# Clustered attention and a gated layer: fp16 hi/lo halves for the cluster logits of pairs 1 to 3, with a new order of pieces

## The chip, the cores and the metric

The kernel runs on one core of a Trainium2 chip. The metric is the device time of one execution in microseconds (us); lower is better. A core has five engines that run side by side and wait for one another through semaphores: TensorE (PE, matmuls into PSUM), VectorE (DVE), ScalarE (ACT), GpSimd (POOL) and SyncE (SP, which here only issues DMAs). Each engine takes its own instructions strictly in the order in which the program issued them.

## The reference

Four batches of eight heads, 768 positions, head dimension 64. Each query and each key is assigned to the nearest of 16 centroids of its head, by the largest cosine; a query sees only the keys of its own cluster. The result, with the heads side by side, is the input of a gated layer.

```python
q_assign = np.argmax(np.einsum('bhsd,hcd->bhsc', q_n, c_n), axis=-1)
k_assign = np.argmax(np.einsum('bhsd,hcd->bhsc', k_n, c_n), axis=-1)
mask = q_assign[:, :, :, None] == k_assign[:, :, None, :]
scores = np.where(mask, scale * np.matmul(q, k.transpose(0, 1, 3, 2)), -1e9)
attn = softmax(scores)                  # rows
x = (attn @ v).transpose(0, 2, 1, 3).reshape(3072, 512)
out = (1 / (1 + np.exp(-(x @ w_gate))) * (x @ w_val)) @ w_out     # 512 -> 1536 -> 512
```

q, k, v and the weights come as fp32. An argmax depends only on the direction of a query, so q and k need not be divided by their norms; but it needs more than fp16's precision where two centroids are close.

## The kernel before, in words

**Heads, pairs and steps.** Heads are worked in pairs (b, p), p from 0 to 3. The attention is a sequence of 384 steps, 96 for each batch. In a step, `do_scores` multiplies one block of 128 keys with 384 queries (`sc`, one PSUM bank of the four of `ring`), and ACT takes the exp of it (`es`, L554). Some steps later, `do_av` multiplies `es` with the values (`av`, L567; `ahead` is 4 in the first batch). At a head's end DVE and POOL divide by the row sums (`normalise`), and the result goes to `xT`, turned by PE or by a DMA.

**The mask is in the matmul.** The tile `T` of a head has 80 rows: 64 of q and k, turned so that the head dimension lies on the partitions, and 16 rows of one-hot cluster numbers. On the key side such a row is 1 in the key's cluster, on the query side it is a large negative number in every cluster but the query's own. So a score of unequal clusters comes out very negative, and exp makes it 0.

**Two ways to the cluster numbers.** The first batch has no time for the slow way, and turns q and k on PE in fp32 (`head`): `f_turn` (`t`, L691, three turns of 128x128 for each head and side, two positions of 64 numbers in each), `f_copy` (`e`, to the fp32 tile `T32`), `f_logits` (`g`, L720, fp32 matmuls with the block-diagonal centroids `cbd`), and `f_half` (`h`, L683, two fp16 casts of 64 partitions from `T32` into `T`). Then `PT`/`PA`/`PB` (L732, L738) find the maximum and mark it, `TT` turns the one-hot rows on PE (L402), and `d` places them in `T` (L749, L751). Batches 1 to 3 (`pair_prep`) split each number into two fp16 halves, hi (L852, a cast) and lo (L858, the number less hi), side by side in a tile `hl`; a DMA transposes `hl` into `T`, so that hi and lo lie under each other, and the logits are fp16 matmuls with the centroids' own hi and lo (`cm`, L352), of which a copy and an addition make the sum (L358, L381).

**Order.** The order of issue is written out by hand in the table `A`. Each piece of work has a name and a place in steps (negative: ahead of the first step; in `pair_prep`, counted from the pair's own first step). `item` puts a piece at the later of its own place and those of the pieces that it builds on; `run_bg(n)` issues the pieces of step n after its scores. A name with an E at the end gives the engine: D is DVE, P is POOL, A is ACT. `dum` are matmuls of zeros that keep PE running at the start, `dn` how many. `w` and `wo` are the weights' loads, which POOL issues; q, k, v are loaded through SP's queue, into four buffers each.

**PSUM.** `prep_bank` takes one of two banks (`op`) for turns, one-hots and value sums as long as the gated layer hasn't begun (before step 96); `bank` takes one of `ring`, which scores and logits share.

**The gated layer.** `ffn_push` queues the layer's matmuls for half a batch (`g` L420, `v` L435, `o` L452), and `ffn_run` spreads them between the steps. The first half of the first batch is due at step 80; what is left runs after the last step.

Of the kernel before, what the change touches and what calls it, by code (L numbers as in the profile page):

```python
# [9 lines left out]
HP = mybir.dt.float16  # L10
# [6 lines left out]
def kernel(  # L17
# [35 lines left out]
    hlp = pool("hl", 4)  # L53
# [21 lines left out]
    def prep_bank(n=512, dt=FP, name="bank"):  # L75
# [9 lines left out]
        "1.0.h00": -54.3, "1.0.l00": -66.6, "1.0.h01": -55.4, "1.0.l01": -60.7, "1.0.tn0": -55.3,  # L85
        "1.0.lg0": -29.3, "1.0.pk00": -62.4, "1.0.pk01": -48.1, "1.0.pk02": -43.9,
        "1.0.pk03": -35.1, "1.0.h10": -50.9, "1.0.l10": -66.6, "1.0.h11": -48.2,
        "1.0.l11": -58.4, "1.0.tn1": -49.0, "1.0.lg1": -25.5, "1.0.pk10": -30.8,
        "1.0.pk11": -58.2, "1.0.pk12": -61.1, "1.0.pk13": -50.3, "1.0.otpe": 0, "1.0.ot": -9.4,
        "1.0.oc": -39.2, "1.0.hop0": -60.3, "1.0.hop1": 1.4, "1.0.vc": -32.4, "1.0.vsm": -19.0,  # L90
        "1.0.vsa": -36.7, "1.0.vsb": -16.9, "1.0.vsr": 1.5, "1.1.ldk": -64.3, "1.1.ldq": -71.6,
        "1.1.ldv": -31.0, "1.1.h00": -40.3, "1.1.l00": -35.9, "1.1.h01": -37.2, "1.1.l01": -84.0,
        "1.1.tn0": -27.6, "1.1.lg0": -20.3, "1.1.pk00": -20.2, "1.1.pk01": -39.9,
        "1.1.pk02": -19.8, "1.1.pk03": -20.7, "1.1.h10": -39.0, "1.1.l10": -31.1,
        "1.1.h11": -36.5, "1.1.l11": -46.2, "1.1.tn1": -22.7, "1.1.lg1": -16.3,
        "1.1.pk10": -14.1, "1.1.pk11": -25.3, "1.1.pk12": -39.8, "1.1.pk13": -46.7,
        "1.1.otpe": 0, "1.1.ot": -12.4, "1.1.oc": -7.2, "1.1.hop0": -34.8, "1.1.hop1": -13.6,
        "1.1.vc": -45.9, "1.1.vsm": -33.5, "1.1.vsa": -26.6, "1.1.vsb": -2.7, "1.1.vsr": 11.6,
        "1.2.ldk": -56.8, "1.2.ldq": -74.0, "1.2.ldv": -49.0, "1.2.h00": -67.9, "1.2.l00": -56.0,
        "1.2.h01": -61.1, "1.2.l01": -48.3, "1.2.tn0": -37.8, "1.2.lg0": -19.8,  # L100
        "1.2.pk00": -29.9, "1.2.pk01": -16.6, "1.2.pk02": -33.0, "1.2.pk03": -19.0,
        "1.2.h10": -37.0, "1.2.l10": -32.1, "1.2.h11": -60.1, "1.2.l11": -34.3, "1.2.tn1": -29.9,
        "1.2.lg1": -15.8, "1.2.pk10": -17.4, "1.2.pk11": -30.5, "1.2.pk12": -15.7,
        "1.2.pk13": -25.1, "1.2.otpe": 0, "1.2.ot": -28.0, "1.2.hop0": -24.1, "1.2.hop1": -29.9,
        "1.2.vc": -46.6, "1.2.vsm": -26.4, "1.2.vsa": -1.2, "1.2.vsb": -19.0, "1.2.vsr": 8.1,
        "1.3.ldk": -73.1, "1.3.ldq": -70.8, "1.3.ldv": -86.1, "1.3.h00": -71.8, "1.3.l00": -72.4,
        "1.3.h01": -61.5, "1.3.l01": -51.2, "1.3.tn0": -49.1, "1.3.lg0": -35.6,
        "1.3.pk00": -36.6, "1.3.pk01": -59.5, "1.3.pk02": -51.9, "1.3.pk03": -30.3,
        "1.3.h10": -53.4, "1.3.l10": -40.6, "1.3.h11": -55.4, "1.3.l11": -55.9, "1.3.tn1": -75.1,
        "1.3.lg1": -20.4, "1.3.pk10": -25.4, "1.3.pk11": -37.4, "1.3.pk12": -18.3,  # L110
        "1.3.pk13": -18.4, "1.3.otpe": 0, "1.3.ot": -11.6, "1.3.hop0": -13.3, "1.3.hop1": -20.5,
        "1.3.vc": -26.2, "1.3.vsm": -11.5, "1.3.vsa": -26.9, "1.3.vsb": -28.2, "1.3.vsr": 4.0,
        "lag0": 8, "lag1": 14, "x0": 56.6, "1.0.h00E": 'P', "1.0.l00E": 'P', "1.0.h01E": 'D',
        "1.0.l01E": 'P', "1.0.h10E": 'P', "1.0.l10E": 'P', "x1": 55.5, "1.0.h11E": 'D',
        "1.0.l11E": 'P', "1.0.mkE": 'P', "x2": 49.1, "1.1.h00E": 'D', "1.1.l00E": 'D',
        "1.1.h01E": 'P', "1.1.l01E": 'P', "1.1.h10E": 'D', "1.1.l10E": 'D', "x_last": 4,
        "1.1.h11E": 'D', "1.1.l11E": 'D', "reserve": 5000, "1.2.h00E": 'P', "1.2.l00E": 'P',
        "1.2.h01E": 'D', "1.2.l01E": 'D', "1.2.h10E": 'D', "1.2.l10E": 'D', "1.1.mkE": 'P',
        "1.2.h11E": 'P', "1.2.l11E": 'D', "1.3.h00E": 'D', "1.3.l00E": 'P', "1.3.h01E": 'P',
        "1.3.l01E": 'D', "1.2.mkE": 'D', "1.3.h10E": 'P', "1.3.l10E": 'D', "1.3.h11E": 'P',  # L120
        "1.3.l11E": 'P', "1.3.mkE": 'P', "cena": -39.3, "cenb": -42.1, "cenc": -30.2,
        "exp": -27.1, "cend": -28.2, "cene": -7.9, "t00": -34.1, "e00": -44.7, "g00": -28.2,
        "h000": -31.3, "h001": -35.4, "t01": -35.1, "e01": -70.3, "g01": -32.3, "h010": -35.2,
        "h011": -15.9, "pt0": -45.6, "pm00": -25.6, "pm01": -34.0, "tt0": -50.1, "pl00": -20.6,
        "pl010": -33.9, "pl011": -28.3, "t10": -29.6, "e10": -11.5, "g10": -29.0, "h100": -10.0,
        "h101": -4.9, "t11": -23.3, "e11": -3.4, "g11": 2.2, "h110": -11.6, "h111": -38.5,
        "pt1": -40.4, "pm10": 7.4, "pm11": -27.2, "tt1": -26.2, "pl10": -10.6, "pl110": -15.2,
        "pl111": -1.5, "vc0": -30.8, "vs0": 12.8, "t20": 10.4, "e20": -22.8, "g20": 14.4,
        "t21": 9.0, "e21": -29.3, "g21": 11.6, "h220": -12.6, "h221": -1.8, "t30": -2.0,
        "e30": -25.3, "g30": 9.3, "t31": 5.6, "e31": -7.3, "g31": 14.5, "h320": -18.3,  # L130
        "h321": -7.6, "PT1": -3.3, "PA1": 2.9, "PB1": 2.6, "TT1": 19.1, "direct1": 2,
        "d100": -14.6, "d101": 3.1, "d110": -13.8, "d111": -48.3, "vc1": 11.3, "vs1": 17.1,
        "t40": 21.3, "e40": 4.0, "g40": 30.2, "t41": 27.5, "e41": 15.1, "g41": 36.0,
        "h420": 14.0, "h421": 36.5, "t50": 30.5, "e50": 36.7, "g50": 44.2, "t51": 30.1,
        "e51": 33.5, "g51": 21.7, "h520": 27.4, "h521": 36.8, "PT2": 46.5, "PA2": 13.2,
        "PB2": 10.0, "TT2": 39.9, "direct2": 2, "d200": -45.4, "d201": -10.1, "d210": -50.1,
        "d211": -5.0, "vc2": 32.1, "vs2": 51.1, "t60": 42.5, "e60": 37.6, "g60": 47.5,
        "t61": 44.8, "e61": 31.4, "g61": 48.3, "h620": 57.1, "h621": 41.7, "t70": 43.0,
        "e70": 31.0, "g70": 49.0, "t71": 39.8, "e71": 26.7, "g71": 52.4, "h720": 41.6,
        "h721": 33.2, "PT3": 38.3, "PA3": 37.5, "PB3": 56.2, "TT3": 35.7, "direct3": 2,  # L140
        "d300": -29.5, "d301": -8.8, "d310": -20.2, "d311": 22.7, "vc3": 51.8, "vs3": 65.5,
        "e00E": 'D', "e01E": 'A', "h000E": 'A', "h001E": 'P', "h010E": 'D', "h011E": 'D',
        "pl00E": 'D', "pl010E": 'P', "pl011E": 'P', "vc0E": 'A', "e10E": 'A', "e11E": 'A',
        "h100E": 'D', "h101E": 'D', "h110E": 'P', "h111E": 'A', "pl10E": 'D', "pl110E": 'D',
        "pl111E": 'P', "cut": 2, "e20E": 'A', "e21E": 'D', "e30E": 'A', "e31E": 'D', "vc1E": 'P',
        "h220E": 'P', "h221E": 'P', "h320E": 'P', "h321E": 'P', "e40E": 'D', "e41E": 'A',
        "e50E": 'D', "e51E": 'D', "vc2E": 'P', "h420E": 'P', "h421E": 'P', "h520E": 'D',
        "h521E": 'D', "e60E": 'A', "e61E": 'A', "e70E": 'D', "e71E": 'D', "vc3E": 'P',
        "h620E": 'P', "h621E": 'P', "h720E": 'A', "h721E": 'P', "xm2E": 'D', "xm3E": 'A',
# [8 lines left out]
        "dum0": -40, "dum1": -30.5, "dum2": -27.9, "dum3": -33.5, "dum4": -31.5, "dum5": -33,  # L158
        "dum6": -27.6, "dum7": -30.9, "dum8": -23.6, "dum9": -20, "dum10": 6.2, "dum11": -0.9,
        "dum12": 0.1, "dn0": 12, "dn1": 0, "dn2": 2, "dn3": 1, "dn4": 0, "dn5": 3, "dn6": 4,  # L160
        "dn7": 3, "dn8": 3, "dn9": 3, "dn10": 1, "dn11": 0, "dn12": 0,
# [228 lines left out]
    def new_oh():  # L390
        oh_n[0] += 1
        return ohs[oh_n[0] % 3]
# [140 lines left out]
    def rows(s):  # L533

        b, p, e = s["b"], s["p"], s["e"]
        if b:
            return {(b, p, f"hop{e}")}
        h = 2 * p + e
        if p == 0:
            i = s["c0"] // 3  # L540
            return {f"h{h}{x}{y}" for x in range(2) for y in range(2)} | {
                f"pl{e}0", f"pl{e}10", f"pl{e}1{i}"}
        d = {f"d{p}{e}{x}" for x in range(2)} if e < A.get(f"direct{p}", 2) else {f"hop{p}{e}"}
        return d | {f"h{h}20", f"h{h}21"}
# [191 lines left out]
    def f_mark(h, nh, s, oh):  # L736
# [3 lines left out]
            bcast(mx[:, :, 6 * s : 6 * s + 6], NCL), ALU.is_lt if s else ALU.is_equal,  # L740
        )

    def place(t, ps, slot, c0, n, key, eng):
        src = ps[32 * slot : 32 * slot + 16, 0 : n * 128].rearrange("p (c t) -> p c t", t=128)
        dst = t[64:80, c0 : c0 + n, :]
        if eng is ACT:
# [250 lines left out]
```

## Time and profile before

| | us |
|---|---|
| median of 5 runs | 340.16 (339.14 to 342.49) |
| the profiled execution | 339.52 |
| its span, first to last instruction | 337.5 |
| first exp / first matmul of the gated layer | 13.44 / 53.89 |
| last step's exps / end of the layer | about 280 / 334 |

Busy time of the engines by stretch, in us:

| stretch | PE | DVE | ACT | POOL |
|---|---|---|---|---|
| 0 to 10 | 7.2 | 4.7 | 5.5 | 3.8 |
| 10 to 50 | 38.2 | 28.7 | 32.3 | 23.6 |
| 50 to 110 | 57.4 | 38.5 | 48.6 | 22.3 |

Lines of the profile name the engine, the line of the kernel, the operation and the tiles. A time in a fence is the start in the span or a length, both in us, and the text ahead of each says which; in groups of instructions the mean is in ns. A bracket at the end, or the last column of a group, tells how long the engine stood idle before the instruction and which other instruction ended that. The granted TensorE clock is 1.00 in every stretch.

### The profile page before, as it was taken

The page shows a single profiled execution, that of the slowest core. Times are in us where ns is not written, and L with a number is a line of the kernel's source. Part 1 is how long each engine was busy: PE and PEld are TensorE (multiplying, and loading weights), DVE is VectorE, ACT ScalarE, POOL GpSimd, SP SyncE. Part 2 cuts the span into 40 slices and gives each one's busy share as a digit, 9 for nine tenths or more (in the row PEclk, how much of TensorE's full clock was granted, in tenths as well). Part 3 has the DMA queues.
Part 4 walks back from the last instruction along what each step waited for, and adds up shares of the span by engine and source line. Part 5 has one row for each costly group of instructions (what it writes and reads, how often), then busy time and mean ns, then how long its engine had stood idle before and what let it go on. Part 6 is the DMA issues. An engine that isn't in the chain of part 4 may idle for free.

```text
span 337.5 us, 8262 instructions
## 1 busy us (share of the span) xinstructions
PE 324.1 (96%) x3135; PEld 208.3 (62%) x3135; DVE 173.4 (51%) x428; ACT 231.6 (69%) x537; POOL 110.4 (33%) x196
## 2 busy tenths in 40 slices
PE   7899999979999998999999999999999999999995
PEld 6688866656656665566665666566655665654552
DVE  4657788666754755465454746465442433403230
ACT  4779799868878886678776877778776873322330
POOL 4365834344043554334444243444120110000000
PEclk9999999999999999999999999999999999999999
DMA  7999997985969594869395837433331200002102
GB/s 256 304 259 249 205 156 198 247 138 112 228 84 235 122 213 105 231 180 142 84 251 130 227 78 198 113 72 81 81 84 40 60 14 14 0 31 81 77 0 93
DMA packets 80854, 46.17 MB, mean 137 GB/s; under 512 B 61104, under 2 KB 77744, under 8 KB 80816
## 3 DMA queue, kind: packets, MB, share of 16 engines
q1 hardware_dynamic: 76816, 40.55, 51.1%
q0 software_dynamic: 3712, 4.72, 7.9%
q8 instruction: 24, 0.39, 0.5%
q10 hardware_dynamic: 288, 0.39, 0.3%
q14 instruction: 14, 0.11, 0.1%
HBM read 28.34 MB, written 6.29 MB: 103 GB/s over the span
## 4 chain that ended last, share of the span: by engine, by line
PE 88%; DMA 5%; ACT 2%; DVE 2%; issue 1%; SPq 0%; POOL 0%; ACTq 0%
PE g L420 18%; PE v L435 18%; PE o L452 18%; PE sc L549 17%; PE av L567 9%; PE lg L720 3%; DMA T<-hl 3%; PE lg L352 2%; DMA vraw<-in_v_dram 2%; DMA T<-ohT 1%; PE t_ps L691 1%; ACT es L554 1%; PE oh_ps L402 0%; ACT L783 0%; DVE oh L738 0%
## 5 line engine op out<-in xcount | busy, mean ns | idle before, releaser
L554 ACT ACTIVATE es<-sc 128x384 f16<-128x384 f32 x384 | 171.5, 499 | 41.5 <-PE sc L549 27.9
L549 PE MATMUL sc<-T 80*128 80x384 f16 x384 | 115.4, 327 | 3.1 <-DMA T<-ohT 1.3
L567 PEld LDWEIGHTS <-es 128*128 128x128 f16 x1152 | 81.6, 98 | 45.1 <-issue 1.5
L440 DVE SCALAR_TENSOR_TENSOR hT<-th,v 128x384 f16<-128x384 f32 x96 | 52.9, 552 | 93.5 <-PE av L567 49.9
L567 PE MATMUL av<-va,es 128*128 128x65 f16 x1152 | 97.4, 193 | 0.6 <-ACT es L554 0.5
L420 PE MATMUL g<-xT,wg 128*128 128x384 f16 x384 | 78.1, 325 | 0.1
L435 PE MATMUL v<-xT,wv 128*128 128x384 f16 x384 | 78.1, 325 | 0.0
L452 PE MATMUL o<-wo,hT 128*128 128x512 f16 x288 | 71.1, 378 | 0.7 <-ACT ob L461 0.7
L426 ACT ACTIVATE th<-g 128x384 f32<-128x384 f32 x96 | 47.3, 492 | 34.0 <-PE g L420 16.7
L327 POOL TENSOR_TENSOR xp<-t,rec 128x384 f16<-128x384 f32 (+1 forms) x38 | 26.7, 703 | 109.1 <-DVE rec L326 99.1
L420 PEld LDWEIGHTS <-wg 128*128 128x128 f16 x384 | 37.2, 97 | 21.5 <-issue 0.4
L435 PEld LDWEIGHTS <-wv 128*128 128x128 f16 x384 | 37.3, 97 | 21.2 <-issue 0.7
L452 PEld LDWEIGHTS <-hT 128*128 128x128 f16 x288 | 28.0, 97 | 26.3 <-issue 1.0
L549 PEld LDWEIGHTS <-T 80*128 80x128 f16 x384 | 37.7, 98 | 2.9 <-DMA T<-ohT 1.1
L325 DVE TENSOR_TENSOR t<-av,sv 128x390 f32<-128x390 f32 (+1 forms) x42 | 19.4, 463 | 13.4 <-PE av L567 13.4
L878 POOL TENSOR_SCALAR oh<-oh 128x96 f16<-128x96 f16 x22 | 9.9, 452 | 32.2 <-DVE oh L370 26.5
L284 DVE TENSOR_REDUCE vs<-vraw 128x64 f16<-128x384 f32 x24 | 19.5, 814 | 0.0
L858 POOL TENSOR_TENSOR hl<-qraw,hl 128x384 f16<-128x384 f32 x20 | 18.3, 913 | 2.1 <-DVE hl L852 0.6
L461 ACT ACTIVATE ob<-o 128x512 f32<-128x512 f32 x16 | 9.6, 597 | 13.6 <-PE o L452 13.5
L381 DVE TENSOR_TENSOR lgs<-lg,lglo 128x192 f32<-128x192 f32 x24 | 8.5, 355 | 15.4 <-ACT lglo L358 15.1
L858 POOL TENSOR_TENSOR hl<-kraw,hl 128x384 f16<-128x384 f32 x12 | 11.0, 913 | 8.6 <-DVE hl L852 7.8
L720 PE MATMUL lg<-cbd,T 128*128 128x32 f32 x96 | 12.8, 273 | 0.7 <-DVE cbd L263 0.5
(81 smaller groups left out, 219.5 us busy)
## 6 DMA issues: line engine op xcount, KB each, us to landing
vraw<-in_v_dram SPq DMA_DIRECT2D x16, 384.0 KB, 4.9
out_dram<-ob SPq DMA_DIRECT2D x24, 256.0 KB, 2.3
kraw<-in_k_dram SPq DMA_DIRECT2D x15, 384.0 KB, 4.4
qraw<-in_q_dram SPq DMA_DIRECT2D x15, 384.0 KB, 6.1
wg<-in_moe_w_gate_dram POOLq DMA_DIRECT2D x2, 768.0 KB, 14.9
wv<-in_moe_w_val_dram POOLq DMA_DIRECT2D x2, 768.0 KB, 20.2
wo<-in_moe_w_out_dram POOLq DMA_DIRECT2D x4, 384.0 KB, 18.9
T<-ohT SPq DMA_DIRECT2D x48, 24.0 KB, 1.9
```

The lines of the kernel that those rows point to most:

```text
L284: DVE.tensor_reduce(s[:, e, 0:64], RAW["v", b, p][:, e].rearrange("p c d -> p d c"), AX.X, ALU.add)
L327: eng.tensor_tensor(x, t[..., 0:64], bcast(r, 64), ALU.mult)
L420: PE.matmul(out=g[:, 0:n], lhsT=wg[fc // WQ][:, dc, fc % WQ, :], rhs=xT[:, dc, t0 : t0 + n], start=(dc == 0), stop=(dc == NDC - 1),)
L426: ACT.activation(th[:, 0:n], g[:, 0:n], AF.Tanh, scale=0.5)
L435: PE.matmul(out=w[:, 0:n], lhsT=wv[fc // WQ][:, dc, fc % WQ, :], rhs=xT[:, dc, t0 : t0 + n], start=(dc == 0), stop=(dc == NDC - 1),)
L440: DVE.scalar_tensor_tensor(hT[:, fc, 0:n], st[0][:, 0:n], 1.0, w[:, 0:n], ALU.add, ALU.mult)
L452: PE.matmul(out=o, lhsT=hT[:, fc, bass.ts(t, 128)], rhs=wo[fc // 3][:, fc % 3, :], start=(fc == 0), stop=(fc == NFC - 1),)
L549: PE.matmul(out=sc.rearrange("p (c t) -> p c t", t=128), lhsT=s["k"], rhs=s["q"], start=True, stop=True,)
L554: ACT.activation(es, sc, AF.Exp, scale=SCALE)
L567: PE.matmul(out=av[:, s["c0"] - base + i, :], lhsT=s["es"][:, bass.ts(i, 128)], rhs=VA[b, p][:, e, s["j"], :], start=(first and i == 0), s ...
L720: PE.matmul(out=st0[lgk(h)][:, o : o + 2 * NCL], lhsT=t32(h, s)[:, c, :], rhs=cbd[:, h], start=True, stop=True,)
L858: eng.tensor_tensor(hl[:, :, 64:128], RAW["kq"[side], b, p][:, e], hl[:, :, 0:64], ALU.subtract)
```

## The change

Pairs 1 to 3 of the first batch get a third way (`style1` to `style3`, all 1), in place of `head`: hi and lo as in the later batches, but turned by PE in fp16, six turns for each head and side, one copy out of PSUM straight into `T`, and logits with the centroids' hi and lo summed in PSUM, two matmuls of 16 columns for each 128 positions. `T32` and the halves `h` are not needed for these pairs. Pair 0 keeps its fp32 way.

```diff
-    hlp = pool("hl", 4)
+    hlp = pool("hl", 5)
...
+    def hi(h, c0, c1, eng):
+        if ("hl", h) not in st0:
+            st0["hl", h] = hlp.tile([128, 12, 128], HP, tag="hl", name="hl")
+        r = RAW["kq"[c0 // 6], 0, h // 2][:, h % 2, c0 % 6 : c0 % 6 + c1 - c0]
+        (ACT.copy if eng is ACT else eng.tensor_copy)(st0["hl", h][:, c0:c1, 0:64], r)
+
+    def lo(h, c0, c1, eng):
+        hl = st0["hl", h][:, c0:c1]
+        r = RAW["kq"[c0 // 6], 0, h // 2][:, h % 2, c0 % 6 : c0 % 6 + c1 - c0]
+        eng.tensor_tensor(hl[:, :, 64:128], r, hl[:, :, 0:64], ALU.subtract)
+
+    def turn_a(name, h, c0, n, bk):
+        if (0, h) not in T:
+            T[0, h] = tp.tile([128, 12, 128], HP, tag="T", name="T")
+        ps = st0[name] = bk(NCH * 128, HP, name="t_ps")
+        for i in range(n):
+            PE.transpose(ps[:, bass.ts(i, 128)], st0["hl", h][:, c0 + i, :], identh)
+
+    def turn_b(name, h, c0, n, eng):
+        (ACT.copy if eng is ACT else DVE.tensor_copy)(
+            T[0, h][:, c0 : c0 + n, :].rearrange("p c t -> p (c t)"),
+            st0[name][:, 0 : n * 128],
+        )
+
+    def a_logits(p, s, e):
+        if ("lgA", p) not in st0:
+            st0["lgA", p] = bank(512, name="lg4")
...
+        for c in range(6):
+            for i in range(2):
+                PE.matmul(
+                    out=lg[:, bass.ts(12 * s + 6 * e + c, NCL)], lhsT=t[:, 6 * s + c, :],
+                    rhs=cm[:, h, i, :], start=(n == c == i == 0), stop=(i == 1),
+                    skip_group_check=True,
+                )
...
+    def a_pick(p, s):
+        lg = st0["lgA", p][:, 0:384].rearrange("p (c n) -> p c n", n=NCL)
+        if s == 0:
+            st0["oh", p] = new_oh()
+            st0["mxA", p] = top(lg)
+        mark(lg, st0["mxA", p],
+             [(12 * s, 12 * s + 12, 2, s == 0, oh_view(st0["oh", p], s, 2, 2, 6))])
```

The pieces are named with pair, side and head: `H` hi, `L` lo, `T` turn, `E` copy, `G` logits, so `H100` is hi of pair 1, side k, head 0. Their places and engines in the table are new, and nearly all other places and many engines change with them; of those, the ones that the prediction speaks of:

```diff
-        "e00E": 'D', "e01E": 'A', "h000E": 'A', "h001E": 'P', "h010E": 'D', "h011E": 'D',
-        "h100E": 'D', "h101E": 'D', "h110E": 'P', "h111E": 'A', "pl10E": 'D', "pl110E": 'D',
+        "e00E": 'A', "e01E": 'D', "h000E": 'P', "h001E": 'P', "h010E": 'P', "h011E": 'A',
+        "h100E": 'A', "h101E": 'D', "h110E": 'A', "h111E": 'D', "pl10E": 'P', "pl110E": 'A',
...
-        "vc1E": 'P', "vc2E": 'P', "vc3E": 'P', "xm3E": 'A',
+        "vc1E": 'A', "vc2E": 'A', "vc3E": 'P', "xm3E": 'P',
...
-        "dn0": 12, "dn5": 3, "dn6": 4, "dn7": 3, "dn8": 3, "dn9": 3, "dn10": 1,
+        "dn0": 11, "dn5": 1, "dn6": 1, "dn7": 1, "dn8": 2, "dn9": 2, "dn10": 0,
...
+        "H100": -19, "L100": -16.0, "H101": -6.1, "L101": -8.6, "H110": -13.1, "L110": -17.5,
+        "H111": -7.1, "L111": -18.5, "T100": 6.5, "E100": 5, "G100": 8.5, "T101": 8.5,
+        "E101": 9.1, "G101": 10, "T110": 8.5, "E110": 10, "G110": 11, "T111": 9.5, "E111": 11, "G111": 13,
...
+        "H100E": 'A', "H101E": 'P', "L100E": 'P', "L101E": 'P', "H110E": 'D', "H111E": 'D',
+        "L110E": 'P', "L111E": 'P', "E100E": 'A', "E101E": 'D', "E110E": 'D', "E111E": 'D',
+        "H200E": 'D', "H201E": 'A', "L200E": 'P', "L201E": 'D', "H210E": 'A', "H211E": 'D',
+        "L210E": 'P', "L211E": 'P', "E200E": 'D', "E201E": 'D', "E210E": 'A', "E211E": 'D',
+        "H300E": 'P', "H301E": 'P', "L300E": 'P', "L301E": 'P', "H310E": 'A', "H311E": 'D',
+        "L310E": 'P', "L311E": 'P', "E300E": 'A', "E301E": 'D', "E310E": 'D', "E311E": 'D',
```

Pair (1,0), the first of the next batch, has its hi pieces h00 and h10 and its lo piece l10 moved from POOL to DVE and its h01 from DVE to POOL; pairs (1,1) to (1,3) have nine pieces moved from DVE to POOL and one the other way.

## The prediction

> **What bounds the kernel now.** I read the busy shares first. TensorE is busy 96% of a 337.5 us span, so the first question is what it is busy with where the change is made. The projections begin at 53.89 us (first `g` matmul, step 80 of the attention), so I took busy times from the first exp (13.44) to there: span, then PE, PEld, DVE, ACT, POOL, the clock, the DMA share and GB/s.
>
> ```profile
> PE 324.1 (96%) x3135; PEld 208.3 (62%) x3135; DVE 173.4 (51%) x428; ACT 231.6 (69%) x537; POOL 110.4 (33%) x196
> 13.44:53.70 40.26, 38.36 (x496) 31.45 (x495) 29.25 (x71) 34.65 (x87) 24.06 (x38) 1.00 1.16 222
> ```
>
> Two engines are nearly full there: PE 38.36 and ACT 34.65 of 40.26 us. The chain that ended last gives prices on PE's path (start, length, what), free of the overlap of pipelined matmuls, and PE's timeline gives the fp16 logits that batch 1 already uses:
>
> ```profile
> 18.31 0.36 PE t_ps L691 x3
> 18.93 0.67 PE lg L720 x6
> 23.70 0.34 PE oh_ps L402 x6
> ...
> 48.34 0.45 PE L352 MATMUL lg<-cm,T 128*128 128x32 f16 x12
> 48.64 0.32 PE L549 MATMUL sc<-T 80*128 80x384 f16 x1
> ```
>
> Three fp32 turns take 0.36 us (0.12 each), six records of fp32 logits 0.67 (0.112 each), six fp16 turns 0.34 (0.057 each), and twelve fp16 logits hold the next score up from 48.34 to 48.64 (0.025 each). Then ACT alone, by groups in the same stretch and in its timeline:
>
> ```profile
> L554 ACT ACTIVATE es<-sc 128x384 f16<-128x384 f32 x79 | 33.3, 527 | 5.5 <-PE sc L549 5.1 <-PE av L567 0.2
> 22.26 5.25 ACT L554 ACTIVATE es<-sc 128x384 f16<-128x384 f32 x13 [0.98 <-PE sc L549]
> ```
>
> Thirteen exps back to back take 5.25 us, 0.404 each, though one alone lasts 0.499: an ACT instruction in a stream costs some 0.095 less than its duration. Eighty exps need 32.3 us of 40.26 whatever PE does. ACT idles 5.6 us, 5.1 of them waiting for scores: that is what a faster PE can give back.
>
> Last the two ends of this stretch: PE's wait for the first one-hot turn, and the longest transfer of the chain after step 80.
>
> ```profile
> 9.98 0.50 PE L772 MATMUL oh_ps<-identh,oh 128*64 128x128 f16 x6 [0.79 <-ACT T L683]
> 72.45 0.47 PE L352 MATMUL lg<-cm,T 128*128 128x32 f16 x12 [1.34 <-DMA T<-hl]
> ...
> 63.77 8.64 DMA T<-hl
> ```
>
> **The change part by part.**
>
> *TensorE.* Removed for three pairs: 36 fp32 turns at 0.12 = 4.3 us and 72 records of fp32 logits at 0.112 = 8.1, together 12.4. Added: 72 fp16 turns at 0.057 = 4.1 and 144 fp16 logits at 0.025 = 3.6 (16 columns where the row has 32; I take no discount), together 7.7. PE's path loses 4.6 us before step 80. Eleven warm-up matmuls also go; all but one stand before the first score, where the chain holds three of them (0.43 us).
>
> Here the Trainium skill speaks against the change. "TensorE: Matmul & The Clock Gate", Part 4 (PE-mode transpose), says that a 128x128 turn takes about 275 ns in a kernel, and that turns don't count as work for the clock. By that rule 72 turns cost 19.8 us in place of 4.1: PE would lose nothing and gain 11 us, near 351 us for the kernel. The row says 0.34 us for six of them in a stream with scores on both sides, at a granted clock of 1.00 in every stretch; each record does last 220 ns, but they overlap. I take the row.
>
> *The engines that feed it.* Nearest rows: hi on POOL 0.53, on DVE 0.39 to 0.56, on ACT 0.51 (its 64x384 cast); lo on POOL 0.913, on DVE 0.56; a 768-wide fp16 copy out of PSUM on DVE 0.551 (the 16x768 one-hot copy), on ACT 0.834 (its 128x768 cast). With the engines of the new table:
> - before: ACT 5 copies + 1 half = 3.3 us; DVE 7 copies + 2 halves = 5.8; POOL 9 halves = 7.6
> - after: ACT 4 hi + 3 copies = 4.5; DVE 5 hi + 1 lo + 9 copies = 7.9; POOL 3 hi + 11 lo = 11.6
>
> The values of pairs 1 and 2 move from POOL to ACT, 2 x 0.834. DVE also takes over two casts and a lo of pair (1,0) and gives one cast away, about +0.9. So DVE goes from 29.3 to about 32.3 us of the stretch, POOL from 24.1 to about 25. I cost both at nothing: they stay below PE and ACT. Without that cover, if one in-order queue made a turn late, the price would be its own added 3 us on DVE, or 4 on POOL.
>
> A second rule bears here. "SBUF — State Buffer" (Who interferes with whom) has a DVE cast in a two-port mode and a GpSimd instruction exclude each other for a whole instruction. The trace agrees: the DVE cast at 34.10 lasts 0.83 us beside POOL's 0.83 us product from 33.89, where a cast of kraw mostly lasts 0.35. By the rule, five hi on DVE could each last 0.83: 2 us more, 34.5 of some 39. Still cover, so both sums are the same.
>
> *ACT, the step that decides.* In the stretch it now has, beside the exps: copies E100, E210, E300 and casts vc1, vc2 (5 x 0.834), hi H201, H210, H310 (3 x 0.51), the one-hot part pl110 (taken as 0.48) and two lglo copies as before (0.65 together): 6.8 us less 11 x 0.095 = 5.8. With 32.3 for the exps it is 38.1, against 34.65 now. PE's need on the chain's prices is 37.0 now (80 steps of one score and three value products at 0.255 = 20.4, 78 logit records 8.7, 35 turns 4.2, 24 value sums and 24 one-hot turns 2.8, batch 1's logits and the x turns 0.9) and falls to 32.4. So the bound changes hands: of the 4.6 us that PE gains, at most 40.26 - 38.1 = 2.2 can show. PE still has to stop for the one-hot of each pair (0.43 at 36.8 and 0.54 at 45.4 now), which four banks of scores cover in part; I leave ACT 0.7 us idle. Stretch: 38.8, **-1.5 us**.
>
> *Start.* The fp32 turn of pair 1 before the first score (0.36) and one or two warm-ups (0.1 each) go: -0.5. Against it H100 and h011 now stand on ACT ahead of the copy e10, whose end (9.94) released the first one-hot turn at 9.98: +0.8 if the turn still needs that bank, nothing if not. Bounds -0.9 and +0.8; the row speaks for the same wait, and what PE does meanwhile (g10, five warm-ups) covers some of it: **0.0**. On POOL the lo pieces of pair 1 come ahead of the weights' DMA issues, which ran at 6.81 and 7.79 and now wait till 12 us or later. The weights are wanted at 53.9 and landed 15 to 20 us after their issue: hidden, and raw loads find freer queues. On DVE, hi pieces follow the first placements: nothing. On ACT nothing waits for a load: pair 1's k, q landed at about 8.2 and 9.2, H100 comes after the table load (9.56).
>
> *After step 80.* Batches 1 to 3 issue the same instructions. Eight hi or lo pieces of pairs (1,1) to (1,3) move to POOL on balance, some 5 us, which is only 20 to 50% busy between 55 and 110. Their loads, transposes and hops change places on SP by a few steps each, and the present queue, which stood 7.9 us over two transposes at 37.4, doesn't show how the new order will queue. In PE's row after 54 I count about 3 us of waits (1.34 at 72.45, 0.66 at 68.37, 1.0 between 130 and 140). A reordering can save all of it or add as much; bounds -2 and +1.5. I take **-0.5**, one of the small waits.
>
> *Sum.* -1.5 + 0.0 - 0.5 = -2.0. The profiled execution took 339.52 us (span 337.5 and 2.0 around it), 0.64 under the median of 340.16. So 337.5 against 339.52, and 338.2 against the median.
>
> **The rivals.**
>
> *PE remains the bound.* The chain runs on PE for nine tenths from 18 to 48 us, and ACT's stream of 0.404 may hide slack. Then the 4.6 us show, and ACT's waits go with them: 335.5, or 334.8 with a quicker start. Against it: exps cannot come closer than in the rows above, and the added ACT work is counted by name.
>
> *The transfers are the wall.* The DMA share is 1.16 in this stretch, at 222 GB/s, and pair (1,1)'s logits waited for a transpose that took 8.64 us. If its landing time at 72.4 doesn't move, a front that is 1.5 us earlier makes a wait of 2.8 there, and the kernel stays near 340. Against it: that transpose is queued behind loads which themselves wait for buffers of the front, so it should move along.
>
> *ACT blocks in order (slower).* A hi, E or vc on ACT that reaches the head of its queue before its input is ready holds every exp behind it, and after four scores PE stops too. ACT's work is 38.1, so idle time of over 2.2 us makes the stretch longer than now; it has 5.6 now. If those waits are latency and not PE's load, and 4.5 us stay, the stretch grows by 2.3 and the start by 0.4: 342.9. For it: five 0.83 us pieces in ACT's stream and the copy E100 at step 6.5, when ACT has no lead. Against it: 5.1 of the 5.6 us idle were waits for scores, behind lumps of logits of 0.67 us (twice 1.34) that shrink to 0.30.
>
> *It doesn't do what it says:* excluded in so far as the engines and counts stand in the code; an fp16 turn can't keep fp32's price on these rows.
>
> **How the numbers follow.** ACT takes over as bound, -1 to -3 us: 0.45, of which 0.38 is past 0.5%. PE remains the bound: 0.20, all faster. Transfers are the wall, or later waits eat the gain: 0.20, nearly all within 0.5%. ACT blocks: 0.15, of which 0.11 is slower by over 0.5%. A measurement of this kernel can't tell less than 0.5% (1.7 us) from no change. Faster 0.60, same 0.27, slower 0.13. The likeliest case alone runs from 337.0 to 339.3. The range goes down to 334.8, the PE rival with a quick start, and up to 340.9, the wall with a slower start, leaving most of the blocking case out.
>
> **What would show it.** Right: six fp16 turns in about 0.34 us and twelve fp16 logits in about 0.30 on the chain; ACT about 38 us busy between first exp and first gate, and that stretch near 38.8; chain lines of `es` where PE stood. Wrong: a stretch under 37.5 (ACT has slack that I don't see) or over 40.3 (blocking: look for long idle times of ACT ahead of copies and hi pieces); the wait at 72.45 grown by what the front gained (the wall); first exp later than 13.9 us. A clock under 1.0 would mean that the dropped warm-ups mattered.

## The result: 338.24 us against 340.15, and where the profile says it came from

| | median, us | lowest to highest | runs |
|---|---|---|---|
| before | 340.15 | 337.18 to 343.02 | 51 |
| after | 338.24 | 335.98 to 340.13 | 30 |

The ratio is 0.9949 [0.9932, 0.9966]: 0.5% faster, 1.7 us of 340.15, with an interval that leaves no change out. The forecast was 338.2. What follows shows that this agreement is partly luck: two larger terms of opposite sign probably stand behind it. Runs more than 1.5% above the fastest of their kernel are left out of every ratio and of the table by clock below.

The profiled execution of the kernel after took 338.75 us (span 336.7). Its page, with the engines' busy times and the granted clock in forty slices of 8.4 us:

```profile
span 336.7 us, 8465 instructions
PE 325.0 (97%) x3232; PEld 207.2 (62%) x3232; DVE 172.4 (51%) x425; ACT 234.8 (70%) x542; POOL 116.0 (34%) x206
PEclk9589999999999999999999999999999999999999
```

PE is busy 0.9 us *longer* than before, although 4.6 us of work were taken from it. The third row says why: the second and third slice were granted 0.5 and 0.8 of the clock. The stretch from first exp to first gate of this execution, then the episode of half clock in it (length, then PE, PEld, DVE, ACT, POOL, clock, DMA share, GB/s):

```profile
13.34:54.70 41.36, 38.60 (x608) 30.26 (x607) 29.98 (x76) 37.42 (x91) 25.50 (x39) 0.92 1.05 211
...
9.44:19.68 10.24, 10.24 (x75) 7.99 (x74) 4.80 (x13) 7.19 (x17) 8.77 (x12) 0.50 1.08 362
```

The clock was half from 9.44 to 19.68 us, so this execution alone doesn't show the front at full clock; two runs further down come nearer to it. What it does show are the prices, in PE's timeline behind the episode (start, length, what; the bracket is the idle time before it and what ended that):

```profile
9.29 0.75 PE L839 MATMUL oh_ps<-identh,oh 128*64 128x128 f16 x6 [0.47 <-DVE oh L756]
...
29.57 0.50 PE L778 MATMUL t_ps<-identh,hl 128*128 128x128 f16 x6
29.91 0.33 PE L567 MATMUL sc<-T 80*128 80x384 f16 x1
...
32.15 0.45 PE L795 MATMUL lg<-cm,T 128*128 128x16 f16 x12
32.45 0.32 PE L567 MATMUL sc<-T 80*128 80x384 f16 x1
...
68.04 0.32 PE L567 MATMUL sc<-T 80*128 80x384 f16 x1 [0.81 <-DVE hT L456]
...
71.27 0.34 PE L616 MATMUL x_ps<-identh,xp 128*128 128x128 f16 x3 [0.39 <-POOL xp L343]
```

Six fp16 turns hold the next score up from 29.57 to 29.91, 0.34 us, and twelve logits from 32.15 to 32.45, 0.30: both are the numbers of the sum. The first one-hot turn no longer waits for ACT's copy `e10` but for DVE's `oh`, and starts at 9.29 where it was 9.98. Behind step 80 the two waits that were 0.66 and 1.34 are now 0.81 and 0.39. The chain of waits says what the second of them hangs on:

```profile
62.51 1.30 SPq L363
...
63.86 0.58 SPq L213
...
64.50 5.69 DMA kraw<-in_k_dram
...
70.25 0.50 POOL hl L936
70.75 0.48 POOL xp L343
...
71.27 0.34 PE x_ps L616 x3
```

SP issues a transpose (L363), a load of v (L213), then a load of k; it lands 5.69 us later; POOL's hi cast had stood waiting for it, and behind that cast in POOL's queue stood the product `xp` that PE needs for an x turn. Where the kernel before waited at 72.45 for a transpose of `hl`, this one waits a microsecond earlier for a load. In this execution the first gate came at 54.71, 0.8 us *later* than before, and from there to the end of the span 282.0 us passed, 1.6 less than before (283.6).

### The profile page after: what moved, and what is told of

It is laid out like the page before. It is cut to its first block, busy times and chain, and to the rows that moved or that the text cites. A ratio compares the mean times of both kernels' runs of the same rounds, so it can differ in the third digit from the quotient of the medians.

```text
span 336.7 us, 8465 instructions
## 1 busy us (share of the span) xinstructions
PE 325.0 (97%) x3232; PEld 207.2 (62%) x3232; DVE 172.4 (51%) x425; ACT 234.8 (70%) x542; POOL 116.0 (34%) x206
## 4 chain that ended last, share of the span: by engine, by line
PE 85%; DVE 5%; DMA 4%; ACT 2%; POOL 1%; issue 1%; SPq 1%; DVEq 0%; ACTq 0%
PE v L451 18%; PE o L468 18%; PE g L436 18%; PE sc L567 16%; PE av L585 9%; DMA kraw<-in_k_dram 3%; PE lg L368 2%; DMA T<-hl 1%; ACT es L572 1%; PE lg L738 1%; PE t_ps L778 1%; DVE T L818 1%; PE lg L795 1%; DVE t L341 1%; DVE T L816 1%
## 5 line engine op out<-in xcount | busy, mean ns | idle before, releaser
L567 PE MATMUL sc<-T 80*128 80x384 f16 x384 | 117.4, 331 | 1.7 <-DVE hT L456 0.8
L585 PEld LDWEIGHTS <-es 128*128 128x128 f16 x1152 | 82.5, 98 | 46.2 <-issue 2.2
L942 POOL TENSOR_TENSOR hl<-qraw,hl 128x384 f16<-128x384 f32 x22 | 20.1, 914 | 4.1 <-PE lg L795 2.6
L397 DVE TENSOR_TENSOR lgs<-lg,lglo 128x192 f32<-128x192 f32 x24 | 8.5, 355 | 12.4 <-ACT lglo L374 11.9
L386 DVE TENSOR_TENSOR oh<-lgs,mx 128x96 f16<-128x96 f32 x48 | 11.9, 287 | 0.8
```

Source lines behind the costliest of these rows:

```text
L567: PE.matmul(out=sc.rearrange("p (c t) -> p c t", t=128), lhsT=s["k"], rhs=s["q"], start=True, stop=True,)
L585: PE.matmul(out=av[:, s["c0"] - base + i, :], lhsT=s["es"][:, bass.ts(i, 128)], rhs=VA[b, p][:, e, s["j"], :], start=(first and i == 0), s ...
L942: eng.tensor_tensor(hl[:, :, 64:128], RAW["kq"[side], b, p][:, e], hl[:, :, 0:64], ALU.subtract)
```

## The experiments

Each kernel differs from the one named by table entries or by a few inserted instructions. Ratios are to the kernel before, run beside it on the same chip, with 95% intervals.

**1. The halves without the rest of the new order.** The kernel after, with every table entry of the kernel before; only the new pieces `H`, `L`, `T`, `E`, `G` and the three styles keep the values of the change.

```diff
-        "e00E": 'A', "e01E": 'D', "h000E": 'P', "h001E": 'P', "h010E": 'P', "h011E": 'A',
+        "e00E": 'D', "e01E": 'A', "h000E": 'A', "h001E": 'P', "h010E": 'D', "h011E": 'D',
...
         "style1": 1, "style2": 1, "style3": 1,
         "H100": -19, "L100": -16.0, "H101": -6.1, "L101": -8.6, "H110": -13.1, "L110": -17.5,
...
```

> The kernel before, with the fp16 pieces of pairs 1 to 3 at their new places and engines, and everything else (other places, engines, warm-ups) as before. Theory A, the gain comes from the front, where ACT takes over as the bound: about 1.5 us faster than before (338.6), first gate matmul near 52.4 us in the profile. Theory B, the gain comes from the new order after step 80: within 0.5 us of before (340), with the waits for a transpose near 72 and for hops near 99 and 131 still there. If the pieces need the rest of the new order to fit, slower than before by 1 us or more.

> halves_alone once more, for the number of its runs was small. If its first result holds: ratio 0.988, faster than the changed kernel by some 2 us; then the rest of the new order gives back part of what the halves bring. If it was chance: ratio near 0.995.

Measured in two sets: 0.9883 [0.9832, 0.9934], median 336.27 us of 6 runs, and 0.9902 [0.9865, 0.9939], 336.63 of 9. So the halves by themselves bring 3.3 to 4.0 us, about twice what the whole change brings. The intervals just touch that of the whole change (0.9932 to 0.9966). That the rest of the new order (the other pieces of the front, the warm-ups and the late order together) costs 1.6 to 2.3 us is therefore likely, from two sets that agree, not certain.

Both profiled executions happened to be the slowest of their sets (339.96 and 339.1), so they can't show where the usual run gains. Their stretches from first exp to first gate, both at full clock, are these:

```profile
13.46:52.65 39.19, 35.78 (x610) 28.32 (x608) 30.55 (x80) 35.81 (x88) 30.58 (x47) 1.00 1.13 220
...
12.84:51.85 39.01, 35.62 (x610) 28.33 (x609) 30.38 (x79) 35.63 (x88) 30.51 (x46) 1.00 1.12 227
```

That is 1.3 and 1.4 us less than the 40.45 of the kernel before (13.44 to 53.89), with ACT busy no more than PE: the values of pairs 1 and 2 stay on POOL here. The two executions also show how a run loses. PE's timeline of the second, then its clock (windows as above):

```profile
65.70 0.32 PE L566 MATMUL sc<-T 80*128 80x384 f16 x1 [1.66 <-DVE hT L455]
...
68.59 0.48 PE L566 MATMUL sc<-T 80*128 80x384 f16 x1 [1.28 <-DVE sv L310]
```

```profile
64.00:66.00 2.00, 0.34 (x6) 0.23 (x5) 1.65 (x3) 0.42 (x1) 1.55 (x4) 1.00 1.06 291
...
68.00:70.00 2.00, 1.41 (x8) 0.73 (x8) 1.90 (x7) 0.83 (x2) 2.00 (x4) 0.50 1.06 165
```

This front was early (first gate 51.85), ran into a wait of 1.66 us and then one of 1.28; in the second the clock fell, and it was half from 67.51 to 74.34 us. Step 192 began at 130.6, no earlier than in the kernel after.

**2. The warm-ups back.** The kernel after with the warm-up matmuls of the kernel before, in number and place.

```diff
-        "dn0": 11, "dn5": 1, "dn6": 1, "dn7": 1, "dn8": 2, "dn9": 2, "dn10": 0,
+        "dn0": 12, "dn5": 3, "dn6": 4, "dn7": 3, "dn8": 3, "dn9": 3, "dn10": 1,
...
```

> The changed kernel with the warm-up matmuls of before (numbers and places). Theory C, the dropped warm-ups cost time through the clock, which was 0.50 from 10 to 18 us in the changed kernel's profile: clock back at 1.00 there, first gate matmul 1 to 2 us earlier than 54.7, total near 337.0. Against it (the clock doesn't reach the end, since ACT has work enough and total times of runs with a clock of 0.98 and of 1.00 don't differ): within 0.5 us of 338.2, or later by the 11 matmuls at 0.11, some 0.3 us on the path of the start.

Measured: 0.9925 [0.9902, 0.9949], 337.44 us of 20 runs, 0.8 us under the kernel after; the intervals overlap, so the gain is not shown. What differs is the clock: some half clock (a mean under 0.996; the table by clock below says why) in 7 of these 20 runs and in 21 of 31 of the kernel after, and a mean of 0.985 or less in none of the 20 and in 11 of the 31. The profiled execution kept the full clock. Its stretch, then PE's timeline:

```profile
12.49:53.16 40.67, 36.11 (x608) 28.31 (x607) 31.85 (x79) 38.04 (x93) 26.12 (x41) 1.00 1.11 217
```

```profile
53.16 0.81 PE L435 MATMUL g<-xT,wg 128*128 128x384 f16 x4 [1.07 <-DMA xT<-xp]
...
70.91 0.34 PE L615 MATMUL x_ps<-identh,xp 128*128 128x128 f16 x3 [2.27 <-POOL xp L342]
```

The front came 1.5 us earlier than in the profile of the kernel after (first gate 53.16), and most of that went into a wait behind it: the last line is the wait at 71.27 of the kernel after, 1.9 us longer, and the turn starts only 0.4 us earlier.

**3. The later batches' order back, and alone.** All entries of batches 1 to 3 (names that begin with `1.` or `g.`): set to their old values in the kernel after, and to their new values in the kernel before.

```diff
-        "1.0.h00": -64.3, "1.0.l00": -68.2, "1.0.h01": -57.4, "1.0.l01": -69.3, "1.0.tn0": -55.2,
+        "1.0.h00": -54.3, "1.0.l00": -66.6, "1.0.h01": -55.4, "1.0.l01": -60.7, "1.0.tn0": -55.3,
...
```

> The changed kernel with the places and engines of batches 1 to 3 as before. Theory B: the waits at 72, 99 and 131 come back, and it is some 1.6 us slower than the changed kernel (339.8, ratio to before 0.999). Theory A: only about 0.5 us slower than the changed kernel (338.7, ratio 0.996).

> The kernel before with the new places and engines of batches 1 to 3 alone. Theory B: about 1.6 us faster than before (338.5), the waits at 72, 99 and 131 gone or half. Theory A: 0.5 us faster (339.6). If the late order was made for the new front only: no faster, or slower by new waits near 70 us.

Measured: old order in the kernel after 0.9933 [0.9907, 0.9959], 337.57 us, not told apart from the kernel after (among runs at full clock it is 336.69 us of 6 against 338.25 of 10); new order in the kernel before 1.0089 [1.0059, 1.0118], 3.0 us of 340.15, slower beyond doubt. So nothing shows a gain by the new late order on either base, and without the halves it hurts. PE's timeline of the second run and its clock show a price, though this execution (340.43 us) was the fastest of its 19:

```profile
37.84 0.51 PE L401 MATMUL oh_ps<-identh,oh 128*128 128x128 f16 x6 [1.34 <-DVE oh L737]
...
39.66 0.32 PE L548 MATMUL sc<-T 80*128 80x384 f16 x1 [0.39 <-DVE T L750]
```

```profile
40.00:44.00 4.00, 4.00 (x28) 3.49 (x26) 1.02 (x3) 1.47 (x4) 0.91 (x1) 0.50 1.26 183
```

DVE, which in this order also makes hi and lo of pair (1,0), is late with a one-hot; PE waits 1.34 us, and the clock is half from 39.91 to 50.15. The first gate comes at 58.43. None of the runs of this kernel had a mean clock over 0.985.

The first run shows a front at full clock that is nearly the change's: up to step 30 or so its order is that of the kernel after, and behind that only pieces of the next batch stand otherwise. Its stretch, its first one-hot turn, and its chain:

```profile
12.49:51.93 39.44, 36.11 (x607) 28.26 (x606) 29.69 (x77) 37.80 (x93) 28.13 (x43) 1.00 1.13 229
```

```profile
8.94 0.52 PE L838 MATMUL oh_ps<-identh,oh 128*64 128x128 f16 x6 [0.47 <-DVE oh L755]
```

```profile
58.54 5.41 DMA vraw<-in_v_dram
...
63.97 0.04 DVE vs L299
...
64.04 6.62 DMA T<-hl
...
70.70 0.47 PE lg L367 x12
```

First exp 12.49 in place of 13.44, first gate 51.93 in place of 53.89, so 39.44 us between them in place of 40.45. With the new late order, in the run with the warm-ups back, it was 40.67, of which the last 1.07 were a wait for a transpose of `xp`. So the change's own front at full clock is not pinned down to better than that. The same wait of 0.47 us ahead of the one-hot turn stands here and in the kernel after; in the one the clock fell, in the other it didn't. The chain then lands at 70.66, where before it landed at 72.4: a front 2.0 us earlier moved that landing by 1.7. Even so PE stood 1.62 us at 65.78, behind the load of v that the chain names.

**4. More work on one engine.** Twenty matmuls of zeros on PE (2.1 us), or five copies of 128x384 on ACT (2.0 us at 0.404), spread from step 20 on, in either kernel.

```diff
+    for i in range(20):
+        i_(f"xd{i}", 20 + 2 * i, lambda: dummies(1))
```

```diff
+    scr = const.tile([128, 384], HP, name="scr")
+    for i in range(5):
+        i_(f"xa{i}", 20 + 8 * i, lambda: ACT.copy(scr, warm[:, 0:384]))
```

> The kernel before with 20 more matmuls of zeros, one every second step from 20 to 58, each 0.107 us of PE in a stream: 2.1 us of PE work in the stretch. Theory A (PE is the bound before): about 2 us slower, 342.3, ratio 1.006. If ACT already sets the pace before: within 0.7 us.

> The kernel before with five more copies of 128x384 on ACT, one every eighth step from 20 to 52, about 0.4 us each in a stream: 2.0 us of ACT work in the stretch. Theory A: ACT idles 5.6 us there and takes most of it, under 0.8 us slower (ratio up to 1.002). If ACT sets the pace: 2 us slower, ratio 1.006.

> The changed kernel with the same 20 more matmuls (2.1 us of PE). Theory A (ACT took over as the bound): under 0.8 us slower than the changed kernel, ratio to before 0.995 to 0.997. If PE is still the bound: 2 us slower, ratio near 1.001.

> The changed kernel with the same five more copies on ACT (2.0 us). Theory A: about 2 us slower than the changed kernel, ratio to before near 1.001, first gate matmul 2 us later. If PE is still the bound and ACT has slack: under 0.8 us slower, ratio 0.995 to 0.997.

| | ratio | of 340.15 us |
|---|---|---|
| before, more PE | 0.9972 [0.9945, 0.9999] | -1.0 |
| before, more ACT | 1.0025 [1.0, 1.0049] | +0.9 |
| after, more PE | 0.9973 [0.9951, 0.9995] | -0.9 |
| after, more ACT | 0.9926 [0.99, 0.9952] | -2.5 |

The kernel after stands at -1.7 in this column. So no addition of 2 us to the front makes either kernel 2 us slower, neither PE's to the kernel before nor ACT's to the kernel after, which are the bounds that the prediction names. More work on PE makes the kernel before rather *faster* (the interval ends just below 1), though its first gate comes 2.1 us later (55.98). More ACT work leaves the kernel after no slower. Its stretch, with ACT's copies in it, and a piece ahead of it:

```profile
13.11:53.17 40.06, 36.62 (x608) 28.58 (x607) 30.88 (x76) 38.77 (x96) 25.66 (x39) 1.00 1.11 218
...
9.31:12.72 3.41, 3.41 (x20) 2.83 (x21) 2.56 (x7) 2.86 (x8) 1.93 (x3) 0.50 1.06 396
```

Beside the row of 39.44 above, ACT is busy 1.0 us more and the stretch is 0.6 us longer; the first exp is also 0.6 us later, behind 3.41 us of half clock. But beside the row of 40.67, which has the new late order and no added copies, the stretch is 0.6 us shorter, and the halves alone have 39.0 to 39.2 us with 2 us less work on ACT. So ACT is the fullest engine of the change's front (37.80 of 39.44 us, PE 36.11), but that its work sets the front's length is not shown, and neither addition shows in full at the end.

**5. The loads of the next batch earlier.** If late loads of k, q and v make the waits at 64 to 72 us, issuing them earlier should free what the front gains. Loads of pairs (1,1) to (1,3) are issued 3 to 19 steps earlier (but q of pair (1,2) two steps later where the late order is the old one), with the pieces that use them held where they were; in the kernel after, in the halves alone, and in the kernel before.

```diff
-        "1.1.ldk": -64.8, "1.1.ldv": -31.0, "1.2.ldk": -56.4, "1.2.ldv": -48.9, "1.3.ldk": -72.5,
+        "1.1.ldk": -71, "1.1.ldv": -48, "1.2.ldk": -74, "1.2.ldv": -68, "1.3.ldk": -88,
...
```

> The changed kernel with the loads of k, q, v for pairs (1,1) to (1,3) issued 3 to 19 steps earlier (1.1.ldk 55 to 49, 1.1.ldv 89 to 72, 1.2.ldk 88 to 70, 1.2.ldq 75 to 72, 1.2.ldv 95 to 76, 1.3.ldk 96 to 80, 1.3.ldq 98 to 82), every piece that uses them held at its place. Theory D (a front that is earlier or later by 2 us doesn't reach the end, because POOL and DVE stand in order before casts of loads that SP has issued too late, near 58 to 66 us): the waits for kraw and vraw go, step 100 comes before 67 us, 1 to 2 us faster than the changed kernel (336.5, ratio to before 0.990). Theory A (front length alone): no change, ratio 0.995.

> halves_alone with the same loads moved. Theory D: faster than halves_alone by 1 us or more and less spread, near 335, ratio 0.985. Theory A: as halves_alone, 0.988.

> The kernel before with the same loads moved. Theory D: the waits at 67 to 72 us shrink, about 1 us faster than before (ratio 0.997), less than in the changed kernel since its front comes later. Theory A: ratio 1.000.

Measured: 1.001 [0.9987, 1.0033], 0.9953 [0.9928, 0.9977] and 1.0023 [0.9995, 1.005]. The remedy failed. The kernel after lost what it had gained; the halves alone lost about half (the intervals overlap slightly); the kernel before shows no change that can be told. The wait was not removed but moved. PE's timeline of the kernel after with early loads, then DVE's and POOL's:

```profile
63.66 0.32 PE L566 MATMUL sc<-T 80*128 80x384 f16 x1 [2.60 <-DVE hT L455]
```

```profile
60.36 0.83 DVE L941 TENSOR_TENSOR hl<-qraw,hl 128x384 f16<-128x384 f32 x1 [1.98 <-POOL hl L935]
61.11 2.03 DVE L941 TENSOR_TENSOR hl<-kraw,hl 128x384 f16<-128x384 f32 x2
63.07 0.54 DVE L455 SCALAR_TENSOR_TENSOR hT<-th,v 128x384 f16<-128x384 f32 x1
```

```profile
59.37 1.41 POOL L935 CAST hl<-qraw 128x384 f16<-128x384 f32 x3 [2.99 <-DMA qraw<-in_q_dram]
```

Read from the bottom: the load of q of pair (1,2), now issued among the others, landed late; POOL's hi stood 2.99 us for it; DVE's lo stood 1.98 us for the hi; behind that lo and two more in DVE's queue stood `hT`, the gated layer's product, and PE stood 2.60 us for that. One late load held three engines, because each takes its instructions in order. In the other two kernels with early loads PE stands 2.68 and 2.90 us for `hT` at the same place.

**The front against the end, over ten executions.** Apart from the early loads and from the kernel before with more ACT work (profiled at 347.18 us), the profiled executions give for each kernel the start of the score matmuls of steps 80 and 192, counted from 0, in us:

| | step 80 | step 192 | between |
|---|---|---|---|
| later order old | 51.0 | 127.7 | 76.7 |
| warm-ups back | 51.8 | 129.7 | 78.0 |
| halves alone | 52.3 and 51.7 | 131.5 and 130.6 | 79.2 and 79.0 |
| after, more ACT | 53.0 | 129.4 | 76.4 |
| before | 53.7 | 131.1 | 77.3 |
| after | 54.5 | 130.0 | 75.5 |
| before, more PE | 55.8 | 130.3 | 74.5 |
| after, more PE | 56.2 | 131.0 | 74.9 |
| later order alone | 58.3 | 131.9 | 73.6 |

Step 80 spreads over 7 us, step 192 over 4. A straight line through the ten has step 192 come only 0.31 us later for each microsecond that step 80 is later (95% interval -0.03 to 0.65), so some 0.7 of what a front gains is given back before step 192. From there to step 380 all take 145.2 to 145.4 us. This is a relation over different kernels, not a controlled test of the cause.

**The clock over all runs.** Runs divided by their mean clock (runs in brackets). The execution with more ACT work above has a mean of 0.995 with 3.41 us at half clock in it, and the four profiled executions with a mean of 0.998 or more have none between the first clock record (4 to 6 us into the span) and the last 1.5 us; so the line is drawn at 0.996:

| | clock 0.996 or more | under 0.996 |
|---|---|---|
| before, three sets | 339.02 (66) | 340.68 (102) |
| before, more PE | 338.41 (16) | 341.67 (4) |
| after | 338.25 (10) | 338.35 (21) |
| after, more PE | 338.31 (7) | 338.74 (15) |
| after, more ACT | 337.15 (3) | 337.33 (14) |
| warm-ups back | 337.43 (13) | 338.06 (7) |
| later order old | 336.69 (6) | 338.03 (16) |
| later order alone | none | 343.16 (17) |
| halves alone, both sets | 336.00 (9) | 337.67 (6) |

More than half of the runs of the kernel before have such an episode, and those runs are 1.7 us longer; in the kernel after two thirds have one, and it costs nothing that can be seen. At full clock the change is worth 0.8 us, with an episode 2.3. Matmuls of zeros may have helped the kernel before in this way: 16 of 20 runs then kept the clock, where 66 of 168 did without them.

## Why the prediction was right, point by point

- **The number:** 338.2 against 338.24. Within the sum the terms were not right.
- **TensorE, -4.6 us before step 80:** right in its prices to 0.01 us, and with them the choice of the row over the Trainium skill's 275 ns for a turn ("TensorE: Matmul & The Clock Gate", Part 4). (The sum as it stands, 12.4 less 7.7, gives 4.7.) As time of the front, the 1.5 that the sum let through is near what the halves alone show there (1.3 and 1.4). That their kernel gains 3.3 to 4.0 all told, near the PE rival's 4.6, does not come from a front shorter by as much in the two executions that were profiled.
- **DVE and POOL at nothing:** right for the front. In the stretch of the kernel after POOL was busy 25.50 us (25 said) and DVE 29.98 (32.3 said), far from the 37 to 39 of ACT and PE. The cover didn't reach the queue behind step 80: there a hi on POOL in front of `xp`, or a lo on DVE in front of `hT`, held PE.
- **Start, 0.0:** the fear was needless. The one-hot turn doesn't wait for `e10` any more, and at full clock the first exp came 0.95 us earlier, the lower of the two bounds (-0.9). It did so with the warm-ups back as well, so that their going brought nothing there. In the profile of the kernel after itself, half the clock ate it (13.34).
- **ACT takes over, -1.5 us (the step said to decide):** the count was right, the consequence not shown. With the old late order at full clock ACT was busy 37.80 us (38.1 counted) and the stretch 39.44 (38.8 said, from a row that ends 0.19 us before the first gate; up to the gate it was 40.45), so it gave -1.0 in place of -1.5; with the start, -2.0 at the first gate. With the new late order it was 40.67, no gain. The profile of the kernel after, at half clock for 10 us, has 41.36, and so the bound "over 40.3" was passed in an execution at half clock and says nothing on ACT. Against ACT as the bound speak the halves alone: 2 us less work on ACT, and a front no longer. More work on ACT did not make the kernel slower. ACT doesn't set the end, and that the number came out is luck.
- **After step 80, -0.5:** this is the step that failed. In the profiled pair that part gains 1.6 us, but such a pair measures the front and the order together, for in the table a later front loses less time behind it. Judged by its own experiments the late order shows no gain: set back in the kernel after, the kernel reads 0.7 us faster, which is not shown; put alone into the kernel before, it costs 3.0 us, beyond doubt. All of the new order beside the halves costs some 2 us, of which the warm-ups (0.8) and the late order (0.7) would be most.
- **The rivals.** The wall was underrated at 0.20. "If its landing time doesn't move" was too hard a form of it: the landing moved by 1.7 of 2.0 us with the old late order. Yet in the table some 0.7 of a front's gain is lost behind it. ACT blocking in order did not happen: in the kernel after ACT took 5.89 us for fifteen exps from 25.68 us on, the old rate, and the front at full clock was shorter. What did block in order was DVE and POOL, later.
- **The clock:** the prediction gave the granted clock one sentence. It turned out to be a term as large as any in the sum: 1.7 us between runs of the kernel before. The dropped warm-ups seem to matter to how often it falls and for how long: half clock in 7 of 20 runs with them back and in 21 of 31 without, a mean of 0.985 or less in none and in 11.

**Left open.** Why the halves alone gain 3.0 us at full clock (336.00 against 339.02), when their step 80 came only 1.4 and 2.1 us earlier and some of that is given back: the two executions that were profiled were the slow ones. What sets the length of their front, in which neither ACT nor PE is busy more than 92%. Which late transfer is the wall: k, q and v each appear as the last to land in some run, and moving them earlier made another one late. And why an episode of half clock costs the kernel before 1.7 us and the kernel after next to nothing.

The best kernel that was run is the halves alone, 336.3 to 336.6 us, 1.0 to 1.2% under the kernel before.

## What to carry to other kernels

When a change brings a new method and a new order together, run the method in the old order: here it was worth about twice the pair. A gain at the front must be followed to the next load that queues behind it; look there for an in-order engine on which a cast that waits for a load stands ahead of something that PE needs. And before a gain of half a per cent is explained by engines, divide the runs by the granted clock: dropping idle matmuls at the start may show only in how often the clock falls.

## What the runs showed of the hardware

The granted clock was 1.00 or 0.50 in these traces. Within the kernels the stretches at 0.50 lasted 3.41 us (9.31 to 12.72 in the kernel after with more ACT work), 6.83 (67.51 to 74.34 in the halves alone), 10.24 (9.44 to 19.68 in the kernel after, 39.91 to 50.15 in the late order alone) and 13.65 (7.59 to 21.25 in the kernel after with early loads), all multiples of 3.41 us. The PE waits at the fall were 0.47 us, 1.34 and 0.39, and 1.66 and 1.28. The Trainium skill ("TensorE: Matmul & The Clock Gate", Part 1) has the clock halved after an idle window of about 3.4 us; no wait in these lines is that long, and the same wait of 0.47 us was followed by an episode in one execution and not in another. So the wait alone doesn't decide it. Nor does PE's busy share: in the 3.41 us ahead of the fall in the kernel after PE was busy 2.61 us, and with the late order old 3.41 us with 2.08 busy (8.42 to 11.83) were followed by no fall. What does decide it, these runs don't show.

At half clock work on PE takes the stretch over: in the kernel after PE was busy for all of the 10.24 us, and the first gate came at 54.71 us, where the two runs of nearly its order at full clock have 51.93 and 53.16. Yet its runs with and without an episode end alike, 338.35 and 338.25 us.

The clock of 1.00 given for the first stretch of the kernel before holds only from 4.24 us on, where its clock records begin. Twelve matmuls of zeros ahead of that took 2.74 us, six at 8.38 us took 0.82: the start ran at a lower speed than the row says.
